# Weight conversions between the activation steps of the last feed-forward group: a three-stage kernel (linear attention, feed-forward, mixture of experts) on one core

## The chip, the cores and the metric

One core of a Trainium2 chip runs the whole program. The metric is device microseconds of one execution. The kernel before was timed three times: 743.41, 744.01 and 747.09 us, median 744.01.

## The reference

Three stages follow each other on 3072 tokens (4 sequences of 768) of 384 channels.

```python
# 1: linear attention with a decaying state, 8 heads of 48 channels
y[:, :, t] = einsum('bhd,bhde->bhe', rt, state + einsum('bhd,bhe->bhde', u * kt, vt))
state = wt[..., None] * state + einsum('bhd,bhe->bhde', kt, vt)
# 2: feed-forward, 384 -> 2048 -> 384
h = x @ w_in
x = where(h > 0, h, exp(min(h, 0)) - 1) @ w_out
# 3: top-1 mixture of 8 experts, 384 -> 1024 -> 384
logits = x @ w_gate + modality_bias[modality_id]
e_idx = argmax(logits); gate = max(softmax(logits))
out[token] = gate * (maximum(x @ w1[e], 0) @ w2[e])     # e = e_idx[token]
```

Data and weights come in float32.

## The kernel before

**Numbers in two halves.** Each float32 operand of a matmul is kept as two float16 tensors, a high part (a rounded copy) and a low part (what the rounding left out). A product is three matmuls: high by high, high by low, low by high.

**Groups and units.** The tokens are cut into 12 groups of 256. Stage 2 goes through each group in eight units, u0 to u7, one per 256 of the 2048 hidden channels. Unit n of the whole run issues `ffn_in` (18 matmuls of 128x256 into a PSUM tile `psf`), the activation, and then `ffn_out` of the unit two before (`LAG` = 2: 12 matmuls of 128x384 into `pso`). There are two `psf` buffers. The activation of a unit is a chain over two engines:

- ScalarE (ACT): L545 (exp) and L546 (scale and bias) write the tile `e`;
- VectorE (DVE): L547 joins `e` with `psf` and thereby ends the use of that `psf` buffer;
- ACT: L549 writes the high part into `ring`, which holds four units;
- `lowp` (L550, whose instruction carries the helper's line L336) writes the low part into `ring`. It runs on GpSimd (POOL) for groups 0 to 9 and on DVE for the last two.

**What runs beside the last group.** While the last group (group 11, units 88 to 95) is in stage 2, the table `LST` starts stage 3:

- `load_q(j, q)` loads a quarter q of the weights of block j (768 KB) from the SP queue into one of four staging buffers. `SG[0]` and `SG[1]` are tiles of their own, the other two lie in `wi`, the input weights of stage 2, whose first units are no longer needed.
- `conv_q(j, q)` converts a staged quarter in two halves. Each half is one ACT instruction (L866, high part) and one DVE instruction (L867, low part) of 128x768. It then starts the load of the same quarter of the next block.
- `first_b` (L716 on TensorE, PE, then small DVE steps L724 to L732) finds which tokens the first blocks hold; `moe_gather` (L831) fetches their rows by indirect DMAs that POOL issues; `moe_xm` (L840) transposes them by DMA from the SP queue.
- `logits(g)` (L585) is 12 small matmuls for a finished group; it reads the transposed output of stage 2 of that group.

After stage 2, `moe_h` (L875) and `moe_o` (L895) work off one block of 256 tokens after the other, 14 blocks in all, the last ones under conditions.

**What sets the order.** The instructions are written unit by unit. A scheduler then fixes one static order for each engine, and each engine works in that order: an instruction that waits holds up all behind it on its engine. `tc.issue_after(x)` sets the instructions of its block behind x on x's engine. The table entry `(1, lambda: conv_q(0, 0))` means: at unit u1 of the last group, ahead of that unit's `ffn_in`, convert quarter 0 of block 0.

Of the kernel before, what the change touches and what calls it, by code (L numbers as in the profile page):

```python
# [13 lines left out]
AF = mybir.ActivationFunctionType  # L14
# [35 lines left out]
def _pow2(n):  # L50
    return float(2.0 ** n)
# [6 lines left out]
PH = SX + SWI  # L58
# [28 lines left out]
NU = NF1 // 2  # L87
# [5 lines left out]
GR = [(sum(_GS[:i]), n) for i, n in enumerate(_GS)]  # L93
# [36 lines left out]
def body(ctx, tc, r, k, v, w, u, rk, ul, w_in, w_out, mod, w_gate, bias, w1, w2, cst, out, dbg=None):  # L130
    nc = tc.nc
# [54 lines left out]
    nel = cp.tile([128, 1], F32, name="nel")  # L186
# [148 lines left out]
    def lowp(lo, f, hi, pool=True):  # L335
        (nc.gpsimd if pool else nc.vector).tensor_tensor(lo, f, hi, op=ALU.subtract)  # L336
# [190 lines left out]
        else:  # L527
            nc.vector.scalar_tensor_tensor(Uf, Uf, _pow2(-KS_), pf, op0=ALU.mult, op1=ALU.add)

    def ffn_in(g, u_):  # L530
        ph = psum("f")
        xg = xT[g]
        mm = None
        for z_ in range(2):
            n = 0
            for kk in range(KD):
                for a, b_ in LOHI:
                    mm = nc.tensor.matmul(  # L538
                        ph[:, 256 * z_:256 * z_ + 256], lhsT=wi[:, u_, a, kk, 128 * z_:128 * z_ + 128],
                        rhs=xg[:, b_ * KD + kk, :], start=(n == 0), stop=(n == 3 * KD - 1),  # L540
                    )
                    n += 1
        MK[0] = mm.ins
        e = b2.tile([128, 512], F32, tag="e", name="e")
        nc.scalar.activation(e, ph, AF.Exp, scale=_pow2(-PH))  # L545
        nc.scalar.activation(e, e, AF.Identity, scale=_pow2(PH), bias=nel)  # L546
        LASTV[0] = nc.vector.scalar_tensor_tensor(e, e, 0.0, ph, op0=ALU.min, op1=ALU.max).ins  # L547
        hl = ring[:, (g * NU + u_) % RING].rearrange("p a m t -> p a (m t)")
        LASTA[0] = nc.scalar.activation(hl[:, 0], e, AF.Copy).ins  # L549
        lowp(hl[:, 1], e, hl[:, 0], g < len(GR) - 2)  # L550

    MK, LASTV, LASTA = [None], [None], [None]
    po_ = {}
# [272 lines left out]
    def moe_gather(j):  # L826
        idx = FT["idx"] if j < NB else FT["idx2"]
        g_ = G[j % 3]
        nr = NT if j >= NB else NF * 128
        for t in range(2):  # L830
            nc.gpsimd.indirect_dma_start(  # L831
                out=g_[:, t, :], out_offset=None, in_=scr[0:nr],
                in_offset=bass.IndirectOffsetOnAxis(ap=idx[:, 0, 2 * j + t:2 * j + t + 1], axis=0),
                bounds_check=nr - 1, oob_is_err=False,
            )
# [8 lines left out]
        et = FT["evi"][0:1, j:j + 1] if j < NB else FT["evi2"][0:1, j:j + 1]  # L844
        return nc.sync.value_load(et, min_val=0, max_val=E - 1)

    def moe_w(j, q, e, part):
        st = SG[q]
        if part == 0:
            if q < 2:  # L850
                nc.sync.dma_start(st, w1[ds(e, 1), q].rearrange("e p x -> p (e x)"))
            else:
                nc.sync.dma_start(st, w2[ds(e, 1), q - 2].rearrange("e p x -> p (e x)"))
            return
        if q < 2:
            dst = W1[j % 2][:, :, :, 512 * q:512 * q + 512]
            sv, sc = st.rearrange("p (k f) -> p k f", k=KD), SW1
        else:
            dst = W2[j % 2][:, :, 4 * (q - 2):4 * (q - 2) + 4, :]
            sv, sc = st.rearrange("p (k f) -> p k f", k=4), SW2  # L860
        for z_ in range(2):
            if q < 2:
                o_, i_ = dst[:, :, :, 256 * z_:256 * z_ + 256], sv[:, :, 256 * z_:256 * z_ + 256]
            else:
                o_, i_ = dst[:, :, 2 * z_:2 * z_ + 2, :], sv[:, 2 * z_:2 * z_ + 2, :]
            nc.scalar.activation(o_[:, 0], i_, AF.Copy, scale=_pow2(sc))  # L866
            nc.vector.scalar_tensor_tensor(o_[:, 1], i_, _pow2(sc), o_[:, 0], op0=ALU.mult, op1=ALU.subtract)  # L867
# [50 lines left out]
    def load_q(j, q):  # L918
        if q == 0:
            RG[j] = moe_reg(j)  # L920
        moe_w(j, q, RG[j], 0)

    def conv_q(j, q, load=True):
        if CV.get(j, 0) > q:
            return
        CV[j] = q + 1
        with tc.issue_after(END["ib"]) if j in (NB - 1, NB) else ExitStack():
            moe_w(j, q, None, 1)
        if load:
            load_q(j + 1, q)  # L930
# [123 lines left out]
    def pre(key):  # L1054
# [4 lines left out]

    LST = (  # L1060
        (0, lambda: (load_q(0, 0), load_q(0, 1))),
        (1, lambda: conv_q(0, 0)),
        (2, lambda: (conv_q(0, 1), load_q(0, 2), moe_gather(0))),
        (3, lambda: moe_gather(1)),
        (4, lambda: (load_q(0, 3), conv_q(1, 0), moe_xm(0))),
        (5, lambda: conv_q(0, 2)),
        (6, lambda: (conv_q(1, 1), moe_xm(1))),
        (7, lambda: (conv_q(0, 3), moe_gather(2))),
        (8, lambda: conv_q(1, 2)),
    )  # L1070
    n_ = 0
    for o in ORD:
        if o == "P":
# [5 lines left out]
    NG = len(GR)  # L1079
    LU = (NG - 1) * NU  # L1080
    for n in range(NG * NU + LAG):
# [27 lines left out]
            with tc.issue_after(LASTV[0]), tc.issue_after(LASTA[0]):  # L1109
                setup2()  # L1110
        l_ = n - LAG - RL
        if l_ >= 0 and l_ % NU == NU - 1 and l_ // NU < NG - 1:
            logits(l_ // NU)
        if l_ > 0 and l_ % (2 * NU) == 2 * NU - 1 and l_ // (2 * NU) < NTL // RT_ - 1:
            route(l_ // (2 * NU))
        for q in range(NTL // RT_ - 1):
# [12 lines left out]
        if n < NG * NU:  # L1129
            if g == 0:  # L1130
                pre((0, u_))
            ffn_in(g, u_)
        if n >= LAG:
            g, u_ = divmod(n - LAG, NU)
            if g == 0:
# [110 lines left out]
```

## Time and profile before

| what | value |
|---|---|
| median of the runs shown | 744.01 us |
| the profiled execution | 748.82 us |
| span of its trace | 747.1 us |
| PE busy (matmuls) | 707.1 us, 95% |
| DVE busy | 507.6 us, 68% |
| ACT busy | 490.5 us, 66% |
| POOL busy | 425.1 us, 57% |
| last group in stage 2, on PE | about 478 to 521 us |
| stage 3 alone | about 521 us to the end |

Times of the trace are microseconds from the start of the span. A line gives the engine, the line of the kernel, the operation, and written tile `<-` read tiles. A busy PE is one with a matmul under way; matmuls overlap, so the start of one group to the start of the next is what it really took.

### The profile page before, as it was taken

Reading aid. Unit: us, or ns where it says so; the run is one execution under the profiler, and the core shown is the slowest. Engines: PE = TensorE matmul, PEld = TensorE weight load, DVE = VectorE, ACT = ScalarE, POOL = GpSimd, SP = SyncE. Lnnn points to the kernel's source line nnn. Section 1 sums busy time; section 2 is a strip of 40 time slices with the busy share of each in tenths; the row PEclk is TensorE's granted clock in tenths of the full one; section 3 lists DMA queues with packets and bytes.
Section 4 is the critical chain, followed back from the end, with each engine's and each line's share of the span. In section 5 each row is a group of like instructions: output and inputs, shape, how many; then the busy total and the mean of one; then the engine's idle time right before and its main releaser. Section 6 shows DMA issues by size and latency. Waiting matters only on the chain. (4 is left out here: it accounts for less than half of the span.)

```text
span 747.1 us, 17657 instructions
## 1 busy us (share of the span) xinstructions
PE 707.1 (95%) x6769; PEld 536.1 (72%) x6769; DVE 507.6 (68%) x1077; ACT 490.5 (66%) x955; POOL 425.1 (57%) x414
## 2 busy tenths in 40 slices
PE   4899989999999999999999999998998999999984
PEld 4768867777777777777777777776776777767763
DVE  5999984575746665667566645777785789666761
ACT  3568755667666677766666765477755977657752
POOL 5878888778677778877767660012053566231221
PEclk9999989999999999999999999999999999999998
DMA  9875343444423442354331202189439999899930
GB/s 296 264 229 189 125 112 81 122 102 112 101 76 91 118 105 58 100 124 102 80 79 55 32 13 33 54 254 303 142 90 329 374 343 333 244 246 238 258 122 13
DMA packets 89059, 114.77 MB, mean 154 GB/s; under 512 B 60709, under 2 KB 67018, under 8 KB 88964
## 3 DMA queue, kind: packets, MB, share of 16 engines
q1 hardware_dynamic: 84512, 102.75, 49.3%
q0 software_dynamic: 3456, 10.24, 4.3%
q8 instruction: 57, 0.93, 0.5%
q10 hardware_dynamic: 996, 0.53, 0.3%
q14 instruction: 38, 0.31, 0.2%
HBM read 90.29 MB, written 9.84 MB: 134 GB/s over the span
## 5 line engine op out<-in xcount | busy, mean ns | idle before, releaser
L538 PE MATMUL psf<-xT,wi 128*128 128x256 f16 x1728 | 212.9, 277 | 6.5 <-DVE e L547 4.6
L562 PE MATMUL pso<-wo,ring 128*128 128x384 f16 x1152 | 211.3, 327 | 0.8 <-ACT wo L301 0.4
L538 PEld LDWEIGHTS <-wi 128*128 128x128 f16 x1728 | 167.1, 99 | 35.3 <-issue 6.4
L562 PEld LDWEIGHTS <-ring 128*128 128x128 f16 x1152 | 110.7, 98 | 63.2 <-issue 2.0
L336 POOL TENSOR_TENSOR ring<-e,ring 128x512 f16<-128x512 f32 x80 | 92.5, 1157 | 55.0 <-ACT ring L549 51.9
L547 DVE SCALAR_TENSOR_TENSOR e<-e,psf 128x512 f32<-128x512 f32 x96 | 65.7, 685 | 83.0 <-ACT e L546 79.3
L895 PE MATMUL pso<-W,gg 128*128 128x384 f16 x624 | 111.0, 326 | 2.3 <-DVE gg L336 2.3
L875 PEld LDWEIGHTS <-W 128*128 128x128 f16 x1008 | 93.6, 99 | 22.8 <-issue 4.2
L549 ACT ACTIVATE ring<-e 128x512 f16<-128x512 f32 x96 | 60.1, 626 | 52.5 <-DVE e L547 52.2
L895 PEld LDWEIGHTS <-gg 128*128 128x128 f16 x624 | 60.1, 98 | 38.6 <-DVE gg L336 4.7
L906 POOL DMA_INDIRECT out_dram<-ob,idxb x20 | 36.2, 1808 | 86.3 <-DVE ob L905 45.4
L545 ACT ACTIVATE e<-psf 128x512 f32<-128x512 f32 x96 | 56.6, 590 | 31.9 <-PE psf L538 27.8
L546 ACT ACTIVATE e<-e,nel 128x512 f32<-128x512 f32 x96 | 69.1, 720 | 2.4
L867 DVE SCALAR_TENSOR_TENSOR W<-SG,W 128x768 f16<-128x768 f32 x56 | 52.3, 956 | 25.6 <-ACT W L866 25.3
L875 PE MATMUL psf<-XM,W 128*128 128x256 f16 (+1 forms) x540 | 61.3, 266 | 0.9 <-ACT mt L881 0.9
L866 ACT ACTIVATE W<-SG 128x768 f16<-128x768 f32 x56 | 45.3, 835 | 21.8 <-DMA SG<-in_w_dram 21.5
L867 DVE SCALAR_TENSOR_TENSOR W<-wi,W 128x768 f16<-128x768 f32 x56 | 52.0, 955 | 8.6 <-ACT W L866 7.4
L336 DVE TENSOR_TENSOR gg<-mt,gg 128x256 f16<-128x256 f32 (+1 forms) x112 | 43.5, 404 | 10.3 <-ACT gg L882 8.8
L866 ACT ACTIVATE W<-wi 128x768 f16<-128x768 f32 x56 | 44.8, 835 | 5.0 <-DMA wi<-in_w_dram 2.0
L882 ACT ACTIVATE gg<-mt 128x256 f16<-128x256 f32 (+1 forms) x112 | 42.6, 400 | 1.7
L350 DVE TENSOR_TENSOR_SCAN RK<-lw,bnd 112x520 f32<-112x520 f32 x24 | 34.5, 1439 | 8.0 <-ACT lw L349 4.6
L881 ACT ACTIVATE mt<-psf 128x256 f32<-128x256 f32 (+1 forms) x84 | 29.1, 360 | 15.8 <-PE psf L875 8.3
(268 smaller groups left out, 1142.4 us busy)
## 6 DMA issues: line engine op xcount, KB each, us to landing
SG<-in_w_dram SPq DMA_DIRECT2D x28, 768.0 KB, 7.0
wi<-in_w_dram SPq DMA_DIRECT2D x28, 768.0 KB, 5.5
stg<-in_w_in_dram SPq DMA_DIRECT2D x8, 768.0 KB, 4.9
stg<-in_w_out_dram SPq DMA_DIRECT2D x8, 768.0 KB, 4.3
ld<-in_rk_dram SPq DMA_DIRECT2D x16, 384.0 KB, 3.2
lw<-in_w_dram SPq DMA_DIRECT2D x24, 227.5 KB, 2.9
lr<-in_r_dram SPq DMA_DIRECT2D x24, 224.0 KB, 3.0
lk<-in_k_dram SPq DMA_DIRECT2D x24, 224.0 KB, 3.0
```

The lines of the kernel that those rows point to most:

```text
L336: (nc.gpsimd if pool else nc.vector).tensor_tensor(lo, f, hi, op=ALU.subtract)
L538: mm = nc.tensor.matmul(ph[:, 256 * z_:256 * z_ + 256], lhsT=wi[:, u_, a, kk, 128 * z_:128 * z_ + 128], rhs=xg[:, b_ * KD + kk, :], start= ...
L545: nc.scalar.activation(e, ph, AF.Exp, scale=_pow2(-PH))
L546: nc.scalar.activation(e, e, AF.Identity, scale=_pow2(PH), bias=nel)
L547: LASTV[0] = nc.vector.scalar_tensor_tensor(e, e, 0.0, ph, op0=ALU.min, op1=ALU.max).ins
L549: LASTA[0] = nc.scalar.activation(hl[:, 0], e, AF.Copy).ins
L562: nc.tensor.matmul(po_[g][i][:, 0:DM], lhsT=hl[:, a, z_, 128 * i:128 * i + 128], rhs=wo[:, u_, b_, z_, :], start=(u_ + z_ + n == 0), stop= ...
L866: nc.scalar.activation(o_[:, 0], i_, AF.Copy, scale=_pow2(sc))
L867: nc.vector.scalar_tensor_tensor(o_[:, 1], i_, _pow2(sc), o_[:, 0], op0=ALU.mult, op1=ALU.subtract)
L875: nc.tensor.matmul(ph[:, 0:n_], lhsT=w_[:, a, kk, 128 * m:128 * m + 128], rhs=xm[:, b_ * KD + kk, 0:n_], start=(n == 0), stop=(n == 3 * KD ...
L882: nc.scalar.activation(h2[:, 0, m, 0:n_], t_, AF.Copy)
L895: MK[0] = nc.tensor.matmul(po[:, 0:DM], lhsT=h2[:, a, m, 128 * t:128 * t + 128], rhs=w_[:, b_, m, :], start=(m == 0 and a + b_ == 0), stop ...
```

## The change

Three edits. First, the conversions of six quarters leave the table and go into `ffn_in` of units u2 to u7 of the last group (`CVU`), in halves: the first half is set behind L546 on ACT, the second behind L549, and both behind L547 on DVE. Quarter 0 of block 0 thereby moves from u1 to u2, quarter 1 of block 0 from u2 to u3; the others keep their unit. Second, `lowp` runs on POOL for all units but the last two of the run, so for 14 more units. Third, `logits` of group 10 goes to u6 of the last group, behind that point's latest matmul (`MK[0]`).

```diff
-    def ffn_in(g, u_):
+    def ffn_in(g, u_, cv=()):
...
-        nc.scalar.activation(e, e, AF.Identity, scale=_pow2(PH), bias=nel)
+        LASTB = nc.scalar.activation(e, e, AF.Identity, scale=_pow2(PH), bias=nel).ins
...
-        lowp(hl[:, 1], e, hl[:, 0], g < len(GR) - 2)
+        if cv:
+            for z_, j in enumerate(cv):
+                for after, z in ((LASTB, 0), (LASTA[0], 1)) if z_ == 0 else ((LASTA[0], 0), (LASTA[0], 1)):
+                    with tc.issue_after(after), tc.issue_after(LASTV[0]):
+                        conv_q(*j, half=z)
+        lowp(hl[:, 1], e, hl[:, 0], g * NU + u_ < NU * len(GR) - 2)
...
-    def conv_q(j, q, load=True):
+    def conv_q(j, q, load=True, half=None):
+        if half is not None:
+            moe_w(j, q, None, 1, (half,))
+            if half == 0:
+                return
+            CV[j] = max(CV.get(j, 0), q + 1)
+            load_q(j + 1, q)
+            return
...
-        (1, lambda: conv_q(0, 0)),
-        (2, lambda: (conv_q(0, 1), load_q(0, 2), moe_gather(0))),
+        (2, lambda: (load_q(0, 2), moe_gather(0))),
         (3, lambda: moe_gather(1)),
-        (4, lambda: (load_q(0, 3), conv_q(1, 0), moe_xm(0))),
-        (5, lambda: conv_q(0, 2)),
-        (6, lambda: (conv_q(1, 1), moe_xm(1))),
-        (7, lambda: (conv_q(0, 3), moe_gather(2))),
+        (4, lambda: load_q(0, 3)),
+        (5, lambda: moe_xm(0)),
+        (6, lambda: moe_xm(1)),
+        (7, lambda: moe_gather(2)),
         (8, lambda: conv_q(1, 2)),
     )
+    CVU = {2: ((0, 0),), 3: ((0, 1),), 4: ((1, 0),), 5: ((0, 2),), 6: ((1, 1),), 7: ((0, 3),)}
...
-        if l_ >= 0 and l_ % NU == NU - 1 and l_ // NU < NG - 1:
+        if l_ >= 0 and l_ % NU == NU - 1 and l_ // NU < NG - 2:
             logits(l_ // NU)
+        if n == LU + 6:
+            with tc.issue_after(MK[0]):
+                logits(NG - 2)
...
-            ffn_in(g, u_)
+            ffn_in(g, u_, CVU.get(u_, ()) if g == NG - 1 else ())
```

On ACT, from the end of u1 on (L549 of u1 is the first row of both pieces). In the rows `W_6975` and `W_6976` are the first-layer weights of blocks 0 and 1, `W_6977` the second-layer weights of block 0; `SG_6969` and `SG_6970` are `SG[0]` and `SG[1]`. Before:

```order
L549 ACTIVATE ring<-e 128x512
L866 ACTIVATE W_6975<-SG_6969 128x3x256 x2
L545 ACTIVATE e<-psf 128x512
L546 ACTIVATE e<-e,nel 128x512
L866 ACTIVATE W_6975<-SG_6970 128x3x256 x2
L549 ACTIVATE ring<-e 128x512
L545 ACTIVATE e<-psf 128x512
L546 ACTIVATE e<-e,nel 128x512
L866 ACTIVATE W_6976<-SG_6969 128x3x256 x2
```

With the change (L866 is now L871):

```order
L549 ACTIVATE ring<-e 128x512
L545 ACTIVATE e<-psf 128x512
L546 ACTIVATE e<-e,nel 128x512
L871 ACTIVATE W_6975<-SG_6969 128x3x256
L549 ACTIVATE ring<-e 128x512
L871 ACTIVATE W_6975<-SG_6969 128x3x256
L545 ACTIVATE e<-psf 128x512
L546 ACTIVATE e<-e,nel 128x512
L871 ACTIVATE W_6975<-SG_6970 128x3x256
L549 ACTIVATE ring<-e 128x512
```

Two conversions in a row ahead of u2's exp have become one between L546 and L549 and one behind L549, and this repeats up to u7.

On POOL, from the last token tile of the attention stage (L510) to the first scatter of results (L911, before L906). Seven low parts stand ahead of the four gathers of blocks 0 and 1, two ahead of those of block 2, one behind them. With the change:

```order
L510 TENSOR_TENSOR x<-y,x 128x384
L336 TENSOR_TENSOR ring<-e,ring 128x512 x7
L836 DMA G_6973<-scr,idxa 128x385 x2
L836 DMA G_6974<-scr,idxa 128x385 x2
L336 TENSOR_TENSOR ring<-e,ring 128x512 x2
L836 DMA wi<-scr,idxa 128x385 x2
L336 TENSOR_TENSOR ring<-e,ring 128x512
L911 DMA out_dram<-ob,idxa 3072x384 x2
```

Before, the same stretch had no low part; the seven end with that of u2, the two are u3 and u4, the last one is u5.

On SP, from the load of quarter 0 of block 1 on. The change puts the load of quarter 1 of block 1 (`SG_6970`) behind the first transpose of gathered rows; before, both loads stood ahead of all transposes of `G`.

```order
L856 DMA SG_6969<-in_w_dram 128x1536
L845 DMA_TRANSPOSE XM_6971<-G_6973 128x6x128
L856 ISA
L856 DMA SG_6970<-in_w_dram 128x1536
L858 ISA
L858 DMA wi<-in_w_dram 128x1536
L845 DMA_TRANSPOSE XM_6971<-G_6973 128x6x128
L845 DMA_TRANSPOSE XM_6972<-G_6974 128x6x128 x2
```

A transpose waits until its gather has landed, and the loads behind it wait with it.

## Rows read from the trace of the kernel before

**Rows 1.** The page, busy time and share of each engine over the span.
```profile
PE 707.1 (95%) x6769; PEld 536.1 (72%) x6769; DVE 507.6 (68%) x1077; ACT 490.5 (66%) x955; POOL 425.1 (57%) x414
```
**Rows 2.** Busy time by stretch: start:end, length, then each engine, granted clock, DMA.
```profile
500.00:520.00 20.00, 17.34 (x130) 12.52 (x129) 15.76 (x27) 15.65 (x27) 7.80 (x6) 1.00 1.09 323
```
**Rows 3.** Who PE waited for from 470 to 560: total, times, longest.
```profile
PE psf L538 <- DVE e L547: 2.7, 2, 1.6
```
**Rows 4.** Timeline of PE: start, length, instruction, count, idle before it and releaser.
```profile
496.14 0.30 PE L585 MATMUL psa<-wg,xT 128*128 128x16 f16 x6
496.65 0.31 PE L585 MATMUL psa<-wg,xT 128*128 128x16 f16 x6 [0.22 <-DMA xT<-X]
...
500.73 2.13 PE L538 MATMUL psf<-xT,wi 128*128 128x256 f16 x18
502.69 2.11 PE L562 MATMUL pso<-wo,ring 128*128 128x384 f16 x12
505.85 2.13 PE L538 MATMUL psf<-xT,wi 128*128 128x256 f16 x18 [1.04 <-DVE e L547]
507.81 2.11 PE L562 MATMUL pso<-wo,ring 128*128 128x384 f16 x12
511.54 2.12 PE L538 MATMUL psf<-xT,wi 128*128 128x256 f16 x18 [1.62 <-DVE e L547]
```
**Rows 5.** Timeline of ACT in the last group.
```profile
491.82 1.58 ACT L866 ACTIVATE W<-SG 128x768 f16<-128x768 f32 x2 [2.81 <-DMA SG<-in_w_dram]
493.31 0.58 ACT L545 ACTIVATE e<-psf 128x512 f32<-128x512 f32 x1
...
502.49 1.58 ACT L866 ACTIVATE W<-SG 128x768 f16<-128x768 f32 x2 [0.66 <-DMA SG<-in_w_dram]
503.98 0.70 ACT L546 ACTIVATE e<-e,nel 128x512 f32<-128x512 f32 x1
...
516.07 1.58 ACT L866 ACTIVATE W<-wi 128x768 f16<-128x768 f32 x2 [1.01 <-DMA wi<-in_w_dram]
```
**Rows 6.** Timeline of the SP queue: first two weight loads, first transposes of gathered rows.
```profile
486.84 1.30 SPq L851 DMA_DIRECT2D SG<-in_w_dram  x2
...
506.83 3.27 SPq L840 DMA_TRANSPOSE XM<-G  x2
```
**Rows 7.** Timeline of POOL: the first and the last of the four gathers of blocks 0, 1.
```profile
500.38 1.79 POOL L831 DMA_INDIRECT G<-scr,idxa  x1 [33.40 <-DVE idta L727]
...
505.50 1.00 POOL L831 DMA_INDIRECT G<-scr,idxa  x1 [0.31 <-issue]
```
**Rows 8.** Instructions by line: shortest/median/longest ns, first and last start, forms.
```profile
L336 POOL TENSOR_TENSOR ring<-e,ring x80: 1144/1157/1177, 48.6 to 446.2; 128x512 f16<-128x512 f32 x80
L336 DVE TENSOR_TENSOR ring<-e,ring x16: 681/692/693, 451.2 to 518.7; 128x512 f16<-128x512 f32 x16
L867 DVE SCALAR_TENSOR_TENSOR W<-SG,W x56: 946/957/976, 492.7 to 714.6; 128x768 f16<-128x768 f32 x56
```
**Rows 9.** Timelines of DVE and POOL: one scan alone, one beside a POOL instruction.
```profile
319.37 1.24 DVE L350 TENSOR_TENSOR_SCAN RK<-lw,bnd 112x520 f32<-112x520 f32 x1
339.64 1.95 DVE L350 TENSOR_TENSOR_SCAN RK<-lw,bnd 112x520 f32<-112x520 f32 x1 [0.67 <-ACT pso L364]
339.50 1.00 POOL L459 TENSOR_TENSOR ld<-ld 128x384 f32<-128x384 f32 x1 [2.29 <-DMA ld<-in_rk_dram]
```
**Rows 10.** The page, DMA issues: count, KB each, median us to landing.
```profile
SG<-in_w_dram SPq DMA_DIRECT2D x28, 768.0 KB, 7.0
```
**Rows 11.** Timeline of POOL in stage 3: the longest gather.
```profile
625.97 4.42 POOL L831 DMA_INDIRECT wi<-scr,idxb  x1 [0.30 <-DVE gg L336]
```
**Rows 12.** Timeline of PE early in stage 3, and one stretch with the granted clock.
```profile
570.00 0.61 PE L875 MATMUL psa<-XM,W 128*128 128x256 f16 x2 [2.65 <-ACT W L866]
570.40 3.56 PE L875 MATMUL psf<-XM,W 128*128 128x256 f16 x18
...
570.00:571.00 1.00, 1.00 (x5) 0.74 (x6) 1.00 (x3) 0.80 (x3) 0.00 (x0) 0.50 1.02 404
```

More of the change, by code (lines that the diff above doesn't have):

```diff
@@ L845, in moe_reg, with moe_w @@
         return nc.sync.value_load(et, min_val=0, max_val=E - 1)
-    def moe_w(j, q, e, part):
+    def moe_w(j, q, e, part, halves=(0, 1)):
         st = SG[q]
@@ L860, in moe_w @@
             sv, sc = st.rearrange("p (k f) -> p k f", k=4), SW2
-        for z_ in range(2):
+        for z_ in halves:
             if q < 2:
```

## The prediction

> **What bounds the kernel now.** I read the page first: PE is busy for 95% of the span [rows 1], so time can only come out of the 40 us in which it is not, and an engine that is relieved elsewhere gives nothing. The busy times by stretch then show where PE idles beside this change: from 500 to 520, the second half of the last group, PE has 17.34 us of work in 20, with ACT and DVE at almost 16 each and the clock at full speed [rows 2]. The waits of PE give the cause: 2.7 us in two pieces for `psf`, released by DVE's L547 [rows 3]. The timeline of PE puts them ahead of u6 and u7, at 505.85 and 511.54, and shows a small wait of the logits for the transposed output in front of them [rows 4].
>
> Why is L547 late? On ACT, the conversion that stands ahead of u2's exp waits 2.81 us for its weights, and the exp behind it starts at 493.31; later the pair at 502.49 stands between an exp and its L546, which then starts at 503.98 [rows 5]. ACT and DVE never catch up, and with two `psf` buffers PE meets the delay four units later. So the bound in this stretch is the order of ACT and DVE, not their total.
>
> **The change part by part.** All sums are made against the profiled execution, 748.82 us with a span of 747.1. It lies 4.8 us above the median of 744.01; differences are carried over to the median.
>
> *What goes.* From start to start, 18 input matmuls take 502.69 - 500.73 = 1.96 us, but the 12 output matmuls 3.16 and 3.73 before u6 and u7 (505.85 - 502.69 and 511.54 - 507.81) [rows 4]. Twelve output matmuls without a wait take no more than the 18, so 1.2 + 1.8 = 3.0 us are lost, a little more than the idle that is listed. The wait of the logits adds 0.22 [rows 4]. Together 3.2 us.
>
> Does the new order remove them? One conversion half on ACT is 0.79 us (1.58 for two [rows 5]). The first fills the time in which ACT waits for L547, the second lies between L549 and the next exp. A unit then costs ACT one exp of 0.58, one L546 of 0.70 [rows 5], one L549 (taken like the exp) and two halves: some 3.5 us, against a PE step of 3.9 (two of 1.96). DVE has L547, about the 0.69 of its low part [rows 8], and twice 0.957 [rows 8]: 2.6 us. Both fit. The logits at u6 come more than 8 us after they would have waited; that 0.22 is safe. I take all 3.2.
>
> *What is added on POOL.* Fourteen low parts of 1.157 us replace fourteen of 0.692 on DVE [rows 8]. For group 10 nothing queues behind them but the last attention tile. In the last group the gathers stand between: four of them run from 500.38 to 506.50 now, 6.1 us with the gaps [rows 7], and the low part of u3 is behind all four. They may start after the index steps, and in DVE's order these come behind the first half of the first conversion: 491.82 + 0.79 on ACT + 0.96 on DVE = 493.6; with some 1.5 us for the index steps and POOL's start (an estimate from seven DVE steps that each take less than a fourth of L547, and one start), 495.1. The four end at 501.2, the low part of u3 at 502.4. PE wants it when? The input matmuls of u4 now start where the logits stood, at 496.14; three steps later (input of u4, output of u2, input of u5) it is 496.14 + 3 x 1.96 = 502.0, and the low part is first read by the third of the next output matmuls, 0.3 later: 502.3. So 0.1 us late; the end points are nothing (gathers right after 493.6) and 3.6 us (gathers only 1.8 us earlier than 500.38, by the 12 input and 3 output matmuls that L716 overtakes on PE). I take 0.3. The low part of u5 behind the gathers of block 2 is needed 8 us later still; nothing is taken for it.
>
> DVE and POOL also get in each other's way. A scan on DVE with two inputs in SBUF takes 1.24 us alone, but 1.95 where it starts inside a POOL instruction of 1.00 (339.50 to 340.50) [rows 9]. The conversions' DVE half and POOL's low part are of that kind too. One low part per unit can hold DVE up by 1.157 at most: 2.6 + 1.157 = 3.8 us, still under 3.9, and in turn a conversion can hold the low part of u3 by 0.96; that is inside the 0 to 3.6 above and why I take 0.3 rather than 0.1.
>
> The Trainium skill (SBUF — State Buffer, section on the two separate sides) states this as an exclusive lock: a DVE instruction with two SBUF inputs and a GpSimd instruction shut each other out for a whole instruction. By that rule, if u3's low part meets a conversion it waits the full 0.96, and the sum would be 0.8 us worse. The trace agrees with the lock; rows 9 show 0.71 of delay for 0.86 that was left of the POOL instruction.
>
> *What is late next.* The pair of conversions at 516.07, which waits 1.01 us for its load [rows 5], stays ahead of the first results of `moe_h`. PE now comes 3.2 us sooner. If that load stays where it was, ACT frees `psf` about when PE wants the third buffer; ends: nothing, or 1.0 us. Taken: 0.3.
>
> Sum: -3.2 + 0.3 + 0.3 = -2.6 us. Behind this stretch the order of the work is the same, so the 2.6 us should stay to the end: 744.0 - 2.6 = **741.4 us**, 746.2 in a profiled execution like that before.
>
> **The rivals.**
>
> *Weights still late, gain lost (0.20).* On SP the load of quarter 1 of block 1 now stands behind the first transpose. The gather comes at 495.1; from gather to transpose it took 506.83 - 500.38 = 6.45 us [rows 6, 7], and a transpose is half of 3.27 [rows 6]: the load goes out at 503.2 and lands, by 5.0 us (486.84 to 491.82 [rows 5, 6]) to 7.0 (the median [rows 10]), at 508.2 to 510.2. ACT wants it in u6, whose input matmuls start at 502.0 + 0.3 + 1.96 + some 0.3 for the logits = 504.6, at 504.6 + 1.96 + 0.58 + 0.70 = 507.8 and would wait up to 2.4 us; u6's low part is read at about 512.4 (four steps after 504.6), which 510.2 + 0.79 + 0.58 + 0.69 = 512.3 just reaches. Each us beyond 7.0 goes to PE; with 10 us to land, nothing is left: **744**.
>
> *Slow gathers (0.08), the rival on the other side.* POOL's gathers now stand ahead of low parts. The longest took 4.42 [rows 11]. Four of that length and three gaps of 0.31 are 18.6 us instead of 6.1; the low part of u3 would come 12.5 us later: 744.0 - 3.2 + 12.6 + 0.3 = **753.7**. It eats the gain from a mean of 2.0 us per gather (2.8 us more than 6.1), and makes the kernel slower by over 0.5% from 2.9. For it: the DMA engines are full here (1.09 [rows 2]). Against: they were full in the same stretch before, and the first took 1.79, the last 1.00 [rows 7].
>
> *More than the last group (0.12).* At 570.00 PE waits 2.65 us for weights that come at the end of the routing chain, and then runs at half clock (0.50, the 1.2 GHz level), 18 matmuls in 3.56 instead of 2.13 [rows 4, 12]. If DVE, freed of low parts, brings that chain forward more than PE, 2.65 + 1.4 go as well: 741.4 - 4.1 = **737.3**. Against: the chain begins with the last group's output, which shifts with PE.
>
> *The longer low part on the path (0.03).* Each low part takes 1.157 us on POOL and took 0.692 on DVE [rows 8], a ratio of 1.67. If PE felt the 0.465 us of difference in each of the 14 units, 6.5 us would come on top: 744.0 - 3.2 + 6.5 = **747.3**. Against: POOL stood idle for 33.40 us before its first gather [rows 7], and the ring leaves a low part two units of time. The Trainium skill (GPSIMD Engine Reference, section on engine selection) states the rule behind this: elementwise work with two inputs belongs on VectorE, as GPSIMD is about twice as slow at it; the trace agrees with the direction, at 1.67.
>
> *The edit does not do what it says (0.02).* If the waits of PE came from late loads alone and not from the order on ACT, **744**. Of the long waits on ACT only the 2.81 us are for a load [rows 5].
>
> **How the numbers follow.** Forecast 0.55, rivals 0.20, 0.08, 0.12, 0.03, 0.02. The range 738.0 to 745.3 takes in the forecast's bounds (all of 3.2: 740.8; both upper ends at once, 3.6 and 1.0, are 745.4), the first and last rival, the spread of 0.6 to 3 us of the runs shown, and leaves out most of the third and the upper part of the second. About 0.5%, 3.7 us, is what a measurement of this kernel can tell from no change. Faster by more (under 740.3): the third rival and a fifth of the forecast, 0.23. Slower (over 747.7): most of the second and a little of the fourth, 0.07. Else 0.70.
>
> **What would show it.** Right: no wait for L547 on PE between 496 and 516; ACT's rows alternate L546, conversion, L549, conversion; POOL's gathers start near 495; the low part of u3 ends near 502.4 and PE waits under 1 us before its third output matmul; the transposes of the last output (L377) start about 2.6 us earlier. Wrong: a wait of PE for POOL's `ring` of over 2 us, ACT waiting in u6 or u7 beyond 512, or a changed gap at 570.

## The result, and the profile after

The change made the kernel slower: 751.86 us (746.43 to 756.37, 22 runs) against 747.60 (743.41 to 752.10, 22 runs beside it), a ratio of the means of 1.0051 with a 95% interval of 1.0031 to 1.0072. The forecast was 741.4 against the 744.01 of that time, a ratio of 0.9965.

The profiled execution took 753.34 us with a span of 751.0 (before: 748.82 and 747.1). Busy time by stretch (start:end, length, then each engine, granted clock, DMA share, GB/s):

```profile
500.00:520.00 20.00, 17.28 (x137) 12.30 (x136) 13.10 (x19) 12.41 (x19) 7.87 (x7) 0.99 0.98 252
520.00:540.00 20.00, 18.63 (x159) 13.88 (x157) 14.22 (x58) 14.39 (x33) 0.00 (x0) 0.92 0.73 225
```

PE is no busier from 500 to 520 than before (17.34 [rows 2]), though ACT and DVE have 3 us less to do there. Who PE waited for, from 470 to 600 (total, times, longest):

```profile
PE psa L880 <- ACT W L871: 3.1, 1, 3.1
PE psf L880 <- DVE e L547: 2.7, 1, 2.7
PE psf L880 <- ACT mt L886: 1.0, 2, 0.9
```

The 2.7 us for L547 [rows 3] are there again, once instead of twice. The timeline of PE (start, length, instruction, count, idle before it and releaser) shows where:

```profile
500.63 2.13 PE L538 MATMUL psf<-xT,wi 128*128 128x256 f16 x18
502.60 2.23 PE L567 MATMUL pso<-wo,ring 128*128 128x384 f16 x12
504.67 0.45 PE L590 MATMUL psa<-wg,xT 128*128 128x16 f16 x12
504.98 2.13 PE L538 MATMUL psf<-xT,wi 128*128 128x256 f16 x18
...
508.89 2.13 PE L538 MATMUL psf<-xT,wi 128*128 128x256 f16 x18
...
513.45 0.49 PE L880 MATMUL psf<-XM,W 128*128 128x256 f16 x3
...
518.62 0.71 PE L880 MATMUL psf<-XM,W 128*128 128x256 f16 x5 [2.72 <-DVE e L547]
...
520.58 2.72 PE L567 MATMUL pso<-wo,ring 128*128 128x384 f16 x8
523.14 0.38 PE L880 MATMUL psf<-XM,W 128*128 128x256 f16 x2
524.38 1.14 PE L880 MATMUL psf<-XM,W 128*128 128x256 f16 x9 [0.86 <-ACT mt L886]
525.36 0.33 PE L377 MATMUL psa<-id,X 128*128 128x128 f16 x3
```

Up to 513 everything forecast is there: u6 starts at 504.98 and u7 at 508.89 without a wait (505.85 and 511.54 [rows 4]). The first product of stage 3 starts at 513.45, where the kernel before has it at 516.10, and this run was 0.6 us later at the logits of group 9 (466.68 against 466.10): 3.2 us ahead, the sum of the removed terms. Behind that, all of it goes and more, 4.8 us in three pieces: 2.72 us of idle, then output matmuls at a granted clock of 0.50, the 1.2 GHz level (eight in 2.72 us from 520.58, elsewhere 1.46), then 0.86 us. L377 starts at 525.36, 2.1 us later than before (523.28), with 27 products of stage 3 done instead of 36.

DVE and ACT at that place:

```profile
503.13 0.17 DVE L846 COPY GC<-G 128x2 f32<-128x2 f32 x1 [3.52 <-DMA G<-scr,idxa]
503.26 0.69 DVE L547 SCALAR_TENSOR_TENSOR e<-e,psf 128x512 f32<-128x512 f32 x1
...
513.23 0.96 DVE L872 SCALAR_TENSOR_TENSOR W<-SG,W 128x768 f16<-128x768 f32 x1
517.74 0.17 DVE L846 COPY GC<-wi 128x2 f32<-128x2 f32 x1 [3.55 <-DMA wi<-scr,idxa]
517.88 0.69 DVE L547 SCALAR_TENSOR_TENSOR e<-e,psf 128x512 f32<-128x512 f32 x1
```

```profile
518.60 0.63 ACT L549 ACTIVATE ring<-e 128x512 f16<-128x512 f32 x1 [3.43 <-DVE e L547]
519.14 0.83 ACT L871 ACTIVATE W<-wi 128x768 f16<-128x768 f32 x1
522.48 1.58 ACT L871 ACTIVATE W<-wi 128x768 f16<-128x768 f32 x2 [2.52 <-DMA wi<-in_w_dram]
523.96 0.36 ACT L886 ACTIVATE mt<-psf 128x256 f32<-128x256 f32 x1
```

L547 of u7 is not late by itself. Ahead of it in DVE's order stands `moe_xm`'s copy of two gate columns, 0.17 us of work that nothing needs for another 20 us, and it waits 3.55 us for the gather of block 2 (here `wi`, whose space that block reuses). The copy for block 0 had already held up an L547, that of u4, by a wait of 3.52 us at 503.13; there PE had room, since u6 wanted the buffer only at 504.98. Then ACT's conversion (1,2), ahead of the first result `mt`, waits 2.52 us for its load, which lands some 10.4 us behind its issue (5.7 before). The queue of SP shows why loads and blocks come late:

```profile
502.56 1.22 SPq L845 DMA_TRANSPOSE XM<-G  x1
504.05 0.35 SPq L856 DMA_DIRECT2D SG<-in_w_dram  x1
504.61 0.33 SPq L858 DMA_DIRECT2D wi<-in_w_dram  x1
504.99 6.27 SPq L845 DMA_TRANSPOSE XM<-G  x3
511.52 0.37 SPq L856 DMA_DIRECT2D SG<-in_w_dram  x1
512.09 0.33 SPq L858 DMA_DIRECT2D wi<-in_w_dram  x1
```

Halves free the staging tiles later, so the loads (1,1) and (0,3) now go out between the two transposes of block 0, the other transposes follow in one run of 6.27 us, and (1,2) leaves at 512.09 (510.34 before). The last of the three landed after 9.8 us (the same one before: 8.0). The last gather of block 2 issues at 507.93 and lands near 517.7 (508.70 and, after 4.9 us, 513.6 before): against the logits of group 9 it went out 1.3 us earlier than before and landed 3.5 us later.

### The profile page after: what moved, and what is told of

Same layout as the page of the kernel before. It is cut to its first block, busy times and chain, and to the rows that moved or that the text cites. A ratio compares the mean times of both kernels' runs of the same rounds, so it can differ in the third digit from the quotient of the medians.

```text
span 751.0 us, 17671 instructions
## 1 busy us (share of the span) xinstructions
PE 707.2 (94%) x6769; PEld 536.0 (71%) x6769; DVE 504.6 (67%) x1063; ACT 490.9 (65%) x955; POOL 442.8 (59%) x428
## 5 line engine op out<-in xcount | busy, mean ns | idle before, releaser
L567 PE MATMUL pso<-wo,ring 128*128 128x384 f16 x1152 | 213.5, 329 | 2.2 <-POOL ring L336 0.8
L538 PE MATMUL psf<-xT,wi 128*128 128x256 f16 x1728 | 210.5, 275 | 3.8 <-DVE e L547 1.8
L336 POOL TENSOR_TENSOR ring<-e,ring 128x512 f16<-128x512 f32 x94 | 109.0, 1161 | 87.5 <-ACT ring L549 84.3
L547 DVE SCALAR_TENSOR_TENSOR e<-e,psf 128x512 f32<-128x512 f32 x96 | 65.6, 684 | 88.4 <-ACT e L546 84.0
L549 ACT ACTIVATE ring<-e 128x512 f16<-128x512 f32 x96 | 60.2, 627 | 56.2 <-DVE e L547 55.6
L911 POOL DMA_INDIRECT out_dram<-ob,idxb x20 | 36.8, 1839 | 84.8 <-DVE ob L910 45.0
L546 ACT ACTIVATE e<-e,nel 128x512 f32<-128x512 f32 x96 | 69.1, 720 | 2.6
L871 ACT ACTIVATE W<-SG 128x768 f16<-128x768 f32 x56 | 45.7, 835 | 19.6 <-DMA SG<-in_w_dram 18.8
L871 ACT ACTIVATE W<-wi 128x768 f16<-128x768 f32 x56 | 45.1, 836 | 7.2 <-DMA wi<-in_w_dram 3.8
```

Of the source, the lines that this page charges most:

```text
L538: mm = nc.tensor.matmul(ph[:, 256 * z_:256 * z_ + 256], lhsT=wi[:, u_, a, kk, 128 * z_:128 * z_ + 128], rhs=xg[:, b_ * KD + kk, :], start= ...
L546: LASTB = nc.scalar.activation(e, e, AF.Identity, scale=_pow2(PH), bias=nel).ins
L567: nc.tensor.matmul(po_[g][i][:, 0:DM], lhsT=hl[:, a, z_, 128 * i:128 * i + 128], rhs=wo[:, u_, b_, z_, :], start=(u_ + z_ + n == 0), stop= ...
```

## The experiments

**Theory A**: three things that stand in line carry the loss: (1) the gate-column copies ahead of L547 on DVE, (2) the conversion (1,2) ahead of `mt` on ACT, and, from the third run on, (3, called D) the two loads between the transposes of block 0 on SP. **B**: the low parts on POOL, and the DVE and POOL instructions that shut each other out, cost it. **C**: the transfers are late in whatever order.

Single times scatter by some 3 us, and part of that arises before 466 us, in code that is the same but for low parts of group 10. So beside the ratio to before the table has the time on PE from the logits of group 9 (the first L585 or L590 behind 455 us) to the placement of the other tokens (`psa<-ohcb,ohp`, L716 or L721) in the one profiled execution, with the same work in between. One execution per kernel gives no scatter for this column, so a microsecond or two in it is weak evidence. The ratios of e1 to e4, e5 to e8, e9 to e12 and e13 to e15 are each to runs of the kernel before taken beside them.

| run | ratio to before (95%) | logits to placement, us |
|---|---|---|
| before | 1 | 83.5 |
| after | 1.0051 (1.0031 to 1.0072) | 86.2 |
| e1_gc | 1.0050 (1.0012 to 1.0087) | 88.7 |
| e2_cv | 1.0047 (1.0014 to 1.0080) | 88.5 |
| e3_gccv | 1.0035 (1.0000 to 1.0070) | 85.9 |
| e4_lpd | 1.0013 (0.9984 to 1.0043) | 86.6 |
| e5_gccv_xm | 1.0017 (0.9989 to 1.0045) | 83.0 |
| e6_all4 | 1.0034 (1.0005 to 1.0062) | 85.9 |
| e7_b_halves | 1.0014 (0.9988 to 1.0040) | 84.7 |
| e8_b_pool | 1.0029 (1.0000 to 1.0057) | 83.8 |
| e9_late | 0.9987 (0.9958 to 1.0017) | 83.3 |
| e10_b_late | 1.0006 (0.9984 to 1.0027) | 83.2 |
| e11_xm | 1.0087 (1.0055 to 1.0120) | 87.2 |
| e12_b_logits | 1.0012 (0.9986 to 1.0037) | 85.2 |
| e13_before_short | 0.9976 (0.9952 to 1.0000) | 83.3 |
| e14_after_short | 1.0045 (1.0020 to 1.0070) | 85.0 |
| e15_late_short | 0.9953 (0.9923 to 0.9982) | 81.2 |

**e1: the copies moved back.**

```diff
 def moe_xm(j):
-    nc.vector.tensor_copy(GC[j % 4], g_[:, :, DM:XR])
+    if j >= NB:
+        moe_gc(j)                  # the same copy
...
+with tc.issue_after(LASTX[0]):     # the last DVE step of ffn_x2
+    for j in range(NB):
+        moe_gc(j)
```

> Theory A (the gain is given back by two in-order blocks: the gate-column copies of moe_xm, which stand on DVE ahead of the exponential's evacuation of L547 and wait for a gather, and the conversion of weight load (1,2), which stands on ACT ahead of the first moe_h results and waits for its load): with only the copies moved behind the last ffn_x2 result, the wait of psf for DVE at u7 (2.7 us after the change) falls to under 0.5, but ACT still waits for the load (1,2), which lands at about 522.5; TensorE runs out of free psf buffers there and stalls 2 to 3 us instead of 0.9, so the time is within 1.5 us of the changed kernel, ratio to before 1.002 to 1.005. Rival B (low parts on POOL and the port DVE and POOL share): the copy is not the cause, L547 of u7 stays late by 1 us or more and the time is as after the change, 1.005. Rival C (the transfers themselves are late, and whatever waits for them ends the same): 1.004 to 1.006 too, with the whole 3.8 us in the wait for the load.

No wait for L547 is left, and nothing is won. PE now stops for block 0 itself, then for the conversion, whose load lands at 524.6 (ACT):

```profile
517.59 0.49 PE L884 MATMUL psf<-XM,W 128*128 128x256 f16 x3 [3.38 <-DVE ring L336]
...
526.49 2.08 PE L884 MATMUL psf<-XM,W 128*128 128x256 f16 x9 [3.53 <-ACT mt L890]
```

and ACT ahead of it:

```profile
524.59 1.58 ACT L875 ACTIVATE W<-wi 128x768 f16<-128x768 f32 x2 [7.24 <-DMA wi<-in_w_dram]
```

The releaser of the first wait needs reading: DVE's `ring` of 516.82 to 517.50 ends just ahead of it, but this product does not read it. It reads XM, and the second transpose of block 0, issued at 506.5, lands after 11.0 us, at 517.5. The changed kernel itself shows no such wait: its product read block 0 at 513.45, at most 8.5 us behind the issue at 504.99.

**e2: the conversion (1,2) alone** behind the copy of the transposed last output.

```diff
-        (8, lambda: conv_q(1, 2)),
...
 with tc.issue_after(TR[0]):
+    conv_q(1, 2)
     conv_q(1, 3)
```

> Theory A: with only the conversion of load (1,2) moved on ACT behind the copy of the transposed block, the wait of ACT for the load of 2.5 us ahead of the first L886 is gone and the wait of psf for it (0.9) too; the 2.7 us wait for DVE at u7 stays, and some of the half-clock stretch behind it; 1 to 2 us better than the changed kernel, ratio to before 1.002 to 1.004. Rival B: nothing moves, 1.005. Rival C: the wait for the load reappears where the conversion now stands and the time is 1.004 to 1.006.

A miss: the wait for L547 grew to 4.16 us, a new one of 1.62 us for `mt` came at 531.71, and the time did not change.

**e3: both.**

> Theory A: both moved, so neither the 2.7 us wait at u7 nor the 0.9 us behind it is left; TensorE runs from u5's input product to L377 with no gap over 0.5 us, and the time is 4 to 6 us below the changed kernel, ratio to before 0.996 to 0.999 (the forecast gain of 2.6 us would be 0.9965). Rival B: 1.004 to 1.006, as the low parts on POOL and the port are untouched. Rival C: 1.002 to 1.006, with the wait turned up at a product that needs the gathered block or the load.

A miss for theory A as it stood. The wait for L547 and the stall behind the load (1,2) are gone, but the one for block 0 stays, and so does that of 1.62 us for `mt`, now at 532.81:

```profile
513.10 2.76 PE L567 MATMUL pso<-wo,ring 128*128 128x384 f16 x16
518.39 0.80 PE L884 MATMUL psf<-XM,W 128*128 128x256 f16 x3 [2.52 <-DVE ring L336]
518.98 2.74 PE L567 MATMUL pso<-wo,ring 128*128 128x384 f16 x8
```

The instructions on XM with their time to landing, for the transpose issued at 507.7:

```profile
L845 SPq DMA_TRANSPOSE XM<-G x1: 1380/1380/1380, 507.7 to 507.7; - x1
...
DMA to landing us min/median/max: 10.6/10.6/10.6
```

507.7 + 10.6 = 518.3, where PE goes on. This is what made (3) part of theory A. In the changed kernel's own profile only (1) and (2) show as waits of PE.

**e4: the low parts of the last group back on DVE**, all else as changed.

```diff
-lowp(hl[:, 1], e, hl[:, 0], g * NU + u_ < NU * len(GR) - 2)
+lowp(hl[:, 1], e, hl[:, 0], g < len(GR) - 1)
```

> The changed kernel with the low parts of the last group back on DVE and nothing else. Theory A: the copies and the conversion stand where they stood, so both stalls stay: within 1 us of the changed kernel, ratio to before 1.003 to 1.006. Rival B: the gain comes back, 0.996 to 0.999. Rival C: POOL is free earlier by about 2.3 us (two low parts of 1.16 us less ahead of the gathers of block 2), the gather lands that much earlier, and 1 to 2.5 us come back: 1.001 to 1.003.

The ratio is the one C gave, 0.0038 under the changed kernel with intervals that overlap, but the profile has no gain in the stretch: PE waits 1.89 us for XM (second transpose of block 0, 10.9 us), then 2.99 for `mt` behind the load (1,2). The gather of block 2 lands 48.2 us behind the logits (logits at 463.72) instead of 51.1 (517.74 - 466.68):

```profile
511.95 0.17 DVE L846 COPY GC<-wi 128x2 f32<-128x2 f32 x1 [2.27 <-DMA wi<-scr,idxa]
```

Its issue, at 502.54, is 2.4 us earlier against the logits, and it still takes 9.4 us to land. So low parts on POOL delay the issue of that gather, as far as one profile can show it; that its landing is slow they do not explain.

**e5: e3, and on SP both transposes of block 0 ahead of the loads (1,1) and (0,3).**

```diff
-        (4, lambda: load_q(0, 3)),
-        (5, lambda: moe_xm(0)),
-        (6, lambda: moe_xm(1)),
+        (5, lambda: xm_first()),   # moe_xm(0); load_q(1, 1); load_q(0, 3); moe_xm(1); load_q(2, 0)
```

> The copies and the conversion moved as in the third run, and on SP both transposes of block 0 ahead of the weight loads (1,1) and (0,3), which stand between them in the changed kernel. Theory A with the transfer order (D): the second transpose lands 3 to 6 us behind its issue instead of 10.6, the wait of 2.5 us at the first L884 goes, and TensorE has no gap over 1 us from u4 to the first L377; from the logits of the group two in front (466 us) to the end 277 to 279 us, against 280.3 in the third run, 284.3 after the change and 281.0 before; ratio to before 0.995 to 1.000. Rival B (low parts on POOL and the shared port): as the third run, 1.002 to 1.005. Rival C (transfers late whatever the order): the wait shows up at the load (0,3) or (1,1) ahead of an exponential, 1.002 to 1.006.

```profile
512.18 2.76 PE L567 MATMUL pso<-wo,ring 128*128 128x384 f16 x16
514.78 0.49 PE L898 MATMUL psf<-XM,W 128*128 128x256 f16 x3
...
520.98 0.50 PE L377 MATMUL psa<-id,X 128*128 128x128 f16 x6
...
528.92 1.14 PE L898 MATMUL psf<-XM,W 128*128 128x256 f16 x9 [2.88 <-ACT mt L904]
```

Block 0's second transpose, now ahead of the loads, lands after 2.8 us. PE has no wait from u4 to L377, which comes 53.1 us behind the logits (520.98 - 467.86; 58.7 after the change; 57.2 before, where 36 products of stage 3 stand ahead of it and not 27, about 1.0 us more). From the logits to the end it is 277.1 us (745.0 - 467.86), as theory A had it. Then both conversions (1,2) and (1,3) stand in front of `mt`, the second waits 1.15 us for its load, and 2.88 us are lost.

**e6: e5 with the low parts of the last group on DVE.**

> As e5_gccv_xm, with the low parts of the last group on DVE. Theory A with D: the low parts on POOL cost nothing where they are, so within 1 us of e5_gccv_xm, or up to 1 us worse as DVE has 0.68 us more in each unit: 0.995 to 1.001. Rival B: 2 to 3 us better than e5_gccv_xm, 0.993 to 0.998.

L377 comes 52.9 us behind the logits, as in e5: with the order mended, POOL or DVE is the same here, which speaks against B. What made this execution longer is the stall and the clock: the stall is 3.58 us, and PE runs at a granted clock of 0.50 behind it, where in e5 it was 1.00:

```profile
527.88 2.08 PE L898 MATMUL psf<-XM,W 128*128 128x256 f16 x9 [3.58 <-ACT mt L904]
529.75 2.12 PE L918 MATMUL pso<-W,gg 128*128 128x384 f16 x6
```

**e7, e8, e12: one part of the change each, in the kernel before**: the halves, the low parts on POOL, the late logits.

> The kernel before with the conversions in halves alone (low parts and logits as before). Theory A: this is the part that moves the loads (1,1) and (0,3) between the transposes and leaves the copies and the conversion in front, so it carries the loss: 1.002 to 1.005, the waits for L547 at u6 and u7 (2.66 us) gone and a wait for the gather or the load behind u7 in their place. Rival B: without low parts on POOL there is no loss and the forecast gain comes: 0.996 to 0.999.

> The kernel before with the low parts of the last two groups on POOL alone. Theory A: within 0.2% of before, 0.998 to 1.002; the waits for L547 of 2.66 us shrink to 1 to 2.5 (DVE has 0.69 us less in each unit) and the gathers start up to 1.4 us later. Rival B: slower, 1.003 to 1.006, DVE conversions beside a POOL low part at 1.5 to 2.4 us instead of 0.96.

> The kernel before with the logits of the group in front two units later and nothing else. Every theory: the wait of 0.22 us ahead of them goes and nothing else, 0.998 to 1.001.

None reaches the loss of the whole by its ratio, and each interval allows no change; but that of e8 only just does, and it takes in the whole loss too, so POOL's share is not settled by it. Theory A had put the loss on the halves (1.002 to 1.005); e7 does not bear that out. With the halves alone the waits for L547 are gone, but one of 1.75 us for the transposed output comes ahead of the logits, left at their old place, and half clock behind it; the copy then waits only 0.63 us. The late logits alone missed too: the waits for L547 stay at 2.2 us, and PE waits 1.43 and 0.72 us for the high and the low part of u4, which it did not before. With POOL alone the wait moves to the low part of u3, which stands behind the four gathers:

```profile
505.45 1.53 POOL L831 DMA_INDIRECT G<-scr,idxa  x1 [0.30 <-issue]
507.00 1.17 POOL L336 TENSOR_TENSOR ring<-e,ring 128x512 f16<-128x512 f32 x1
```

```profile
508.22 1.80 PE L562 MATMUL pso<-wo,ring 128*128 128x384 f16 x10 [3.33 <-POOL ring L336]
```

That is the place priced in the prediction at 0.1 to 3.6 us. In the whole change it cost 0.1 (the row at 502.60 takes 2.23 instead of 2.11), since the halves start the gathers at 495.34 there and not at 500.94 as here.

**e9: e5 with (1,2) and (1,3) converted behind the fifth and the eighth product of block 0.**

```diff
             moe_h(j, m, 128 * nt)
+            if j == 0 and m in (4, 7):
+                with tc.issue_after(MT[0]):      # the h2 of this m
+                    conv_q(1, 2 if m == 4 else 3)
```

> As e5_gccv_xm, with the conversions (1,2) and (1,3) put on ACT behind the evacuation of the fifth and of the eighth moe_h product of block 0. Theory A with D (each step of the chain gather, transpose, load, conversion waits in line ahead of an evacuation): the stall of 2.88 us behind the logits of the last group goes, no other of over 1 us comes up to 560 us; from the logits of the group two in front (466 us) to the first product behind the gap at 570 us about 101 us, against 103.9 before, 103.9 in e5_gccv_xm and 108.4 after the change; ratio to before 0.993 to 0.998. Rival C (the loads bound this stretch, in whatever order): the loads (2,2) and (2,3) come that much later and the wait at 570 us grows by as much; 0.998 to 1.002.

The best version with full loads, 0.0064 under the changed kernel, with intervals that do not meet, and no better than before by what the interval can tell. From 500 to 520 PE now does what the forecast wanted (17.34 us of work before):

```profile
500.00:520.00 20.00, 19.84 (x165) 14.62 (x164) 15.61 (x22) 15.40 (x25) 7.50 (x6) 1.00 1.10 243
```

The stall of 2.88 us is gone; 1.39 (behind a conversion that waits 1.90 us for its load), 0.72 and 0.94 us come in its place before 549.

**e10: the kernel before with the copies and late conversions of e9.**

> The kernel before with the copies of the gate column and the conversions (1,2) and (1,3) moved as in e9_late. Theory A: little was in line behind them there, so the waits for L547 at u6 and u7 stay within 1 us of their 2.66 us and up to 1.2 us are gained (the wait of 0.83 us ahead of a copy, 0.3 us of psf): 0.997 to 1.001. If these moves are worth as much without the change, 0.993 to 0.997, and the halves add nothing to e9_late.

Nothing gained by what the interval can tell; the moves are worth something together with the change. The waits for L547 shrank to 0.60 us each, which I had not expected.

**e11: the changed kernel with only the order of SP mended.**

> The changed kernel with both transposes of block 0 ahead of the loads (1,1) and (0,3) on SP, and nothing else. Theory A with D: the copies and the conversion still stand in line, so DVE still waits for the gather of block 2 ahead of L547 of u7 and ACT for the load (1,2): 2 to 4 us of psf waits, 1.002 to 1.006. If the order of the transfers alone is the cause: 0.997 to 1.000.

Worst of all: PE waits 1.09 us for L547 and 3.66 us for `mt`. The order of the transfers alone is not the cause.

**e13 to e15: short loads.** In the kernel before, the changed one and e9, the loads of blocks 1 and 2 bring a quarter of their columns; the conversions stay whole. The order written by the scheduler shifts in a few places with it.

```diff
 if part == 0:
+    if j in (1, 2):
+        c = slice(192, 320) if q < 2 else slice(0, 96)
+        nc.sync.dma_start(v[:, :, c], src[:, :, c])     # v, src: staging and weights as (p, k, f)
```

> The kernel before, with the weight loads of blocks 1 and 2 cut to a quarter of their bytes (so the products of those two blocks are not the reference's); conversions and everything else stay. Both theories: the wait for L547 at u6 and u7 (2.7 us) stays, as ACT and DVE do the same work. If the transfers bind the stretch (C): from the logits at 466 us to the placement of the second half (L716) 1 to 2 us less than before's 83.5 us, and the gap at 570 us stays, as its loads are not cut: 0.995 to 0.999. If not: as before, 0.998 to 1.001.

> The changed kernel with the same short loads. If the transfers bind (C): the gathers and the load (1,2) land 3 to 5 us sooner, the waits behind the copy and the conversion shrink below 1 us together, and the change now gains the forecast 2 to 3.2 us over e13_before_short: 79 to 81 us from the logits to L721, against 86.2 in the changed kernel; ratio to before 0.992 to 0.997. If the change costs it by itself: it stays 2 us or more behind e13_before_short.

> e9_late with the same short loads. If the transfers bind (C): as e14_after_short or up to 1 us better, 78.5 to 80.5 us from the logits to L721, against 83.3 in e9_late: 0.991 to 0.996. If the change costs it by itself: 82 us or more.

In e13 the wait for L547 did not stay, as both theories had it: it is 0.49 us, with 1.4 us of small waits for the high and low parts beside it.

C's forecast for e14 failed: with the last gather of block 2 landing after 5.3 us instead of 9.8 the change is still 0.69% over e13, by theory A's first mechanism. Its DVE, then ACT, then PE:

```profile
516.61 0.17 DVE L846 COPY GC<-wi 128x2 f32<-128x2 f32 x1 [1.98 <-DMA wi<-scr,idxa]
```

```profile
517.46 0.63 ACT L549 ACTIVATE ring<-e 128x512 f16<-128x512 f32 x1 [3.31 <-DVE e L547]
```

```profile
518.15 0.82 PE L567 MATMUL pso<-wo,ring 128*128 128x384 f16 x4 [2.28 <-ACT ring L549]
```

But this is not the order of the changed kernel: the scheduler set the copy of block 2 a unit earlier, ahead of the L547 of u6 instead of u7. Here the gather lands 47.0 us behind the logits (516.61 - 469.65); in the changed kernel the L546 of u7 ends at 47.8 (514.44 - 466.68). So, as an estimate, with short loads and the copy left where it was, DVE would not have waited. The wait needs both, a place in line and a late landing, and e14 does not exclude C for the changed kernel.

With the order mended (e15) the change is 0.92% under e14, well outside the intervals, and 2.1 us under e13 in the stretch. By the runs that last step is 0.0023, and the intervals overlap. And e15 has 2.2 us less in the stretch than e9, which differs in the length of the loads alone.

## Why the prediction was wrong

- *What goes: 3.2 us.* Right, at its place and in its size: 3.2 us ahead at the first product of stage 3. That only the order of ACT and DVE made L547 late was too narrow: in single profiles the waits for it also shrink with shorter loads (e13, 0.49 us) and with the copies and late conversions moved (e10, 1.20 us).
- *Both new orders fit a unit.* Right for ACT, whose order was listed; that of DVE was not listed, and the sum left out the two columns' copy. I took DVE's unit as L547 and two halves, and never looked at what `moe_xm` puts there. It was there to be seen: in the kernel before, the first of these copies waits 0.83 us for its gather, ahead of a conversion and an L547:

```profile
508.96 0.17 DVE L841 COPY GC<-G 128x2 f32<-128x2 f32 x1 [0.83 <-DMA G<-scr,idxa]
509.06 1.83 DVE L867 SCALAR_TENSOR_TENSOR W<-wi,W 128x768 f16<-128x768 f32 x2
510.81 0.68 DVE L547 SCALAR_TENSOR_TENSOR e<-e,psf 128x512 f32<-128x512 f32 x1
```

- *Added on POOL: 0.3.* Measured 0.1 for u3's low part, the gathers at 495.34 as forecast (495.1). That two more low parts now stand ahead of the gather of block 2 has no term in the sum; in e4, without them, that gather left 2.4 us earlier.
- *What is late next: 0.3, ends 0 and 1.0, "if that load stays where it was".* This is the step that failed. The load did not stay: it left SP 1.75 us later, and landed later still. I followed one load past the first transpose (the rival of 0.20) and not the other transfers, nor asked when the gather of block 2 and (1,2) land; a wait behind that gather has no term in the sum. Measured in place of the 0.3: 2.72 us of idle for the gather of block 2, by way of its copy ahead of L547, 0.86 us for the load (1,2), and 1.3 us (2.72 - 1.46) of half clock on the eight output matmuls at 520.58 alone. Block 0 was not late in that profile: its first product ran at 513.45 without a wait, and in e5 and e9 PE works through to L377.
- *Behind this stretch the order is the same.* Nearly right: from the placement of the other tokens to the end the two profiles take 198.2 us (751.0 - 552.83) and 197.5 (747.1 - 549.61). The gap at 570 did not close, it was 3.13 us (2.65 [rows 12]), again with half clock behind it. What came out of the stretch was a loss, and that stayed.
- *Rivals.* Weights late had the right queue, but its own load (1,1) went out at 504.05 and the conversion at 509.91 did not wait for it; it ended at 744, with no price for what else goes out late. Slow gathers ended at 753.7, near the right time, by luck: the four gathers ran as forecast (6.4 us with the gaps), and it was the landing of the next block's gather, not the issue of these, that was slow. That POOL's longer low part loses 6.5 us, and that the edit does nothing, both fell.
- *The exclusion of DVE and POOL.* Seen: a conversion takes 2.41 us instead of 0.96 beside POOL's low part, and u6's L549 waits 1.10 us behind it. PE did not feel it in that unit.

```profile
508.80 2.41 DVE L872 SCALAR_TENSOR_TENSOR W<-wi,W 128x768 f16<-128x768 f32 x1 [0.18 <-ACT W L871]
509.21 1.17 POOL L336 TENSOR_TENSOR ring<-e,ring 128x512 f16<-128x512 f32 x1
```

  The conversion ends 0.83 us behind the low part (511.21 and 510.38), as if it had run only after it. The rule of the Trainium skill named there (SBUF — State Buffer, SBUF: two separate sides), that the two shut each other out, agrees with that; why the one that starts first by the trace is the one that waits, no run here shows.

What is shown: in the changed kernel PE stands behind two instructions that wait in line, the copy and the conversion (1,2). Moving one of the three things alone only hands the stall to the next (e1, e2, e11), and moving two leaves stalls (e3). With all three moved, and the conversions set behind results of block 0, the loss is gone (e9 against after); e5, without that last step, is between, with intervals that overlap. The copies and late conversions moved without the change give nothing that the interval can tell (e10). What stays open: the share of each move, and that of the low parts on POOL, for which e4 and e8 speak and e6 does not; the gain of e4 is also not explained by its own profile. Open too is whether shorter transfers alone would have saved the changed kernel in its own order, and what the change is worth with the order mended. The runs allow from 0.42% faster to 0.17% slower with full loads (e9); with short loads the profile says 2.1 us faster, the runs 0.23% faster, with intervals that overlap.

## What to carry to other kernels

A wait that is removed is worth no more than the time until the next operand is late: before summing what goes, write down for each engine that comes earlier when its next operands land (loads, gathers, transposes) and subtract. On engines that work in order, a tiny instruction with a far-off operand is as dangerous as a long one; let the order listing show everything that stands ahead of the evacuation that frees PSUM, not the instructions of the change alone. And a change of the conversions moves the loads that wait for their staging tiles, so the queue must be followed to the end of the stretch.

## What the runs showed of the hardware

- A DMA transpose that goes out behind two loads of 768 KB can land late: block 0's second took 11.0, 10.6 and 10.9 us there (e1, e3, e4), 7.2 in e7, at most 8.5 in the changed kernel, and 2.8 us ahead of the loads (e5). The last gather of block 2 took 9.8 us in the changed kernel, 4.9 before, and 5.3 with loads of a quarter of the length (e14).
- Full queues do not always carry the same: from 500 to 520 the DMA share is 0.98 at 252 GB/s after the change and 1.09 at 323 before. The order of the transposes does not explain it, since e9, with that order mended, has 1.10 at 243.
- Behind a stall of PE the granted clock may fall to 0.50, the 1.2 GHz level: behind 1.75 (e7), 2.28 (e14), 2.52 (e3), 2.72 (the changed kernel), 2.99 (e4), 3.53 (e1), 3.58 (e6), 3.66 (e11, some 1.5 us after PE went on) and 4.16 us (e2) it did, behind 1.39 (e9), 2.88 (e5), 3.33 (e8) and 3.38 us (e1) it did not, so the length alone does not decide. Nine matmuls of 128x256 then take 2.08 us instead of 1.14 (e6). In e7 the 1.75 us of idle were followed by twelve output matmuls in 3.79 us instead of 2.11, so there the stall cost about twice its length.
